# Four single-bank PSUM tiles in place of two double-bank ones, from the end of the attention on

## The chip, the cores and the metric

The kernel runs on one core of one Trainium2 chip. What counts is the device time of one execution in microseconds. The core's engines are TensorE (PE: matmuls, with PEld for its weight loads), VectorE (DVE), ScalarE (ACT), GpSimd (POOL) and SyncE (SP, which here only issues DMAs). TensorE writes its sums into PSUM, of which the kernel uses eight banks of 128 partitions by 512 floats; VectorE and ScalarE read them out.

## What is computed

Attention with capped scores, then two feed-forward layers, all in float32:

```python
scores = cap * tanh(q @ k.T / sqrt(64) / cap)        # 4 x 12 heads, 448 x 448
x = softmax(scores) @ v                              # -> 1792 tokens x 768
h = x @ w_in;  y = (h * cos(h)) @ w_out              # 768 -> 2048 -> 768
a, b = y @ w1, y @ w2                                # 768 -> 1024 each
out = ((a * b) @ w3) @ w_out2                        # 1024 -> 1024 -> 768
```

The product of w3 and w_out2 is formed in the kernel (`make_w34`), so that the last line is one product.

## The kernel before

Every float32 product is made of three matmuls of split operands (`mm3`, lines 378 to 381: high by high, high by low, low by high); a sum collects in one PSUM bank over several `mm3` and is then read out by VectorE or ScalarE. Transposed activations have 448 columns, one batch entry at a time.

The program is written as a list of operations with due times, operands and costs (`Plan.op`), and `Plan.schedule` (lines 191 to 288) works out from them one order for each engine. The order is fixed when the program is built; on the chip an engine takes its list in order, and an instruction waits where its data or its buffer isn't ready. Buffers come from rings: a `Ring` keeps a heap of free slots with the time from which each is free, gives out the one free longest, and takes it back with the end of its last use (lines 236 to 267).

PSUM is held by three rings. Lines 439 to 441 open two tiles of two banks each, `double0` and `double1`, and four tiles of one bank, `bank4` to `bank7`; the list `banks` names the halves of the doubles 0 to 3. `s_r` gives out whole doubles, for the attention's scores: `c_S` (line 590) writes both halves, and `c_exp` (line 602) reads both at once with a Tanh and an Exp (line 607). `pv_r` holds two single banks for the attention's products with v, `hy_r` two for all else. `Plan.move` (line 177) hands a slot from one ring to another: it waits in the plan until the source ring has a free slot, takes it, and puts it, or the slots that `to` names, into the other ring's heap. When the attention ends, `columns` (lines 668 to 670) hands each double to `hy_r` as two banks, as soon as that double is free, and the last `pv_r` bank too; one bank of `pv_r` has gone over earlier (line 667). From then on `hy_r` has all eight banks, four of which are halves of doubles, and Ref-s to them are views of a double (line 440).

The stages overlap: `make_w34` beside the attention, then `moe1` (first layer, units of `mm_h` and `y_part`), begun beside the attention's second half, then `moe2`. `moe2` runs two passes p = 0 and p = 1 over pairs of batch entries. In each, `ab_step` (line 1170) makes, for one block of 128 of the 1024 columns, the two products a and b of two batch entries with seven half-size products (`PRODUCTS`: A11, A12, S2, S1, S3, S4, A22, nine matmuls each) in two banks in turn: products 0, 2, 4, 6 go into p1, 1 into p2, 3 and 5 into p3, each time after the bank was read out (`out` copies, `tt` adds, lines 1183 to 1209). Between them stand the pieces of `o_unit` (line 1213): six sums `acc[m]` that stay in six banks over all eight blocks, three matmuls for each and block. So `ab_step` works with two banks while six are held. In the first pass the right factors (`rights`, line 1123) are converted from raw words first (`convert`, line 819); in the second they are loaded ready.

Pools of tiles are opened and closed in a fixed nesting; the pool `psum` stays open from start to end (lines 437 and 1275).

Of the kernel before, what the change touches and what calls it, by code (L numbers as in the profile page):

```python
# [11 lines left out]
F32 = mybir.dt.float32  # L12
# [4 lines left out]
PSUM = bass.MemoryType.PSUM  # L17
DRAM = bass.MemoryType.DRAM

P = 128  # L20
# [114 lines left out]
class Plan:  # L135
# [38 lines left out]
        self.ops.append(o)  # L174
        return o

    def move(self, src, dst, due, to=None):

        o = Op(due, [(None, 0.0, None)], 0, None)
        it = src.new()  # L180
        it.first = o
        o.allocs.append(it)
        o.move = dst, to or (lambda k: (k,))
        self.ops.append(o)

    def event(self, f, after, before):
        o = Op(-1.0, [(None, 0.0, f)], 0, None)
        self.events.append((o, after, before))
        self.ops.append(o)
# [122 lines left out]
def tile_kernel(tc, *args):  # L312


    nc = tc.nc
    cap = args[3]
    program(tc, *args)
    with tc.tile_pool(name="large", bufs=1) as p:
        c = p.tile([1, 2], F32, name="cap2")
        large = p.tile([1, 1], mybir.dt.int32, name="large")  # L320
        nc.sync.dma_start(c[:, 0:1], cap.rearrange("(o n) -> o n", o=1))
        nc.vector.tensor_scalar(c[:, 1:2], c[:, 0:1], -1.0, None, op0=ALU.mult)
        nc.vector.tensor_tensor(c[:, 0:1], c[:, 0:1], c[:, 1:2], op=ALU.max)
        nc.vector.tensor_scalar(large, c[:, 0:1], CAP_MAX, None, op0=ALU.is_gt)
        with tc.If(nc.values_load(large[0:1, 0:1], min_val=0, max_val=1) > 0):
            program(tc, *args, general=True)
# [3 lines left out]
def program(  # L330
# [12 lines left out]
    general=False,  # L343
# [4 lines left out]
    plan = Plan()  # L348
# [38 lines left out]
    pools = {}  # L387

    def pool(name, **kw):
        pools[name] = Pool(tc, name, {} if general else PADS, **kw)  # L390
        return pools[name]

    right = dict(side="right", reuse_waits="tile")
    for name, kw in dict(const={}, xring={}, dram=dict(space=DRAM), psum=dict(space=PSUM), attn={}, lp={},
                         wi=dict(side="right"), wp=dict(side="right"), yp=right, hp=right, mp=right, cv=right,
                         q2=right).items():
        pool(name, **kw)
# [16 lines left out]
    class Scratch:  # L414
# [7 lines left out]
        def at(self, sub, pick=None):  # L422
            return Ref(self.item, sub, pick)
# [12 lines left out]
    for n in ("const", "xring", "dram", "psum", "attn", "wi", "wp"):  # L436
        pools[n].open()
    psum = pools["psum"].pool
    doubles = [psum.tile([P, 2, 512], F32, name=f"double{n}", bufs=1) for n in range(2)]
    banks = [d[:, n, :] for d in doubles for n in range(2)]  # L440
    banks += [psum.tile([P, 512], F32, name=f"bank{n}", bufs=1) for n in range(4, 8)]
    if general:
        s_r, pt_r, pv_r, hy_r = Banks((0, 1)), Banks((2, 3)), Banks((4, 5)), Banks((6, 7))
    else:
        s_r, pv_r, hy_r = Doubles((0, 1)), Banks((4, 5)), Banks((6, 7))
# [65 lines left out]
    def a_load(i, g):  # L511
        b, h = divmod(i, H)
        qk[i] = A["qr"].new(), A["kr"].new()
        for it, src in zip(qk[i], (q2, k2)):
            for j in range(2):
                r = it.at(j, rows(j))
                dma(at(g) if i else -99.0, r, lambda src=src: src[b, h // 2].rearrange("(i d) s -> d i s", i=2),
                    w=[r], kb=230)
# [6 lines left out]
    def a_split(i, g):  # L525
        q, k = (Ref(x) for x in qk.pop(i))
        qh, ql, ks = (A[x].ref() for x in ("qh", "ql", "ks"))
        copy(at(g), ks, k, 2 * S, "PAD")
        low = Ref(ks.item, None, rows(1))
        lo(at(g), low, k.view(rows(1)), low, 2 * S)  # L530
        copy(at(g), qh, q, 2 * S, "PAD")
        lo(at(g), ql, q, qh, 2 * S)
        for j in range(2):
            st[i + j] = qh[:, j], ql[:, j], ks[:, j]
# [23 lines left out]
    def of_head(f, lag, g, n):  # L558
        i, c = divmod(g - lag, n)
        if c == 0 and 0 <= i < NH:  # L560
            f(i, g)

    def of_pair(f, lag, g, n):
        i, c = divmod(g - lag, n)
        if c == 0 and 0 < i < NH and i % 2 == 0:
            f(i, g)

    def each(f, lag, g, n):
        if 0 <= g - lag < n * NH:
            f(*divmod(g - lag, n), g)  # L570
# [7 lines left out]
    def c_consts():  # L578
        for j in range(2):
            r = A[f"v{j}"]  # L580
            for _, k in r.free:
                POOL.memset(r.tile(k)[:, :, 1 - j, :], 1.0)
# [68 lines left out]
    def columns():  # L651
        c_consts()
        a_load(0, -2)
        a_split(0, -1)
        for g in range(-8, NT * NH + 16):
            of_pair(a_load, -G["ql"], g, NT)
            of_head(cv_load, -2, g, NT)
            of_pair(a_split, -G["qs"], g, NT)
            each(c_S, 0, g, NT)
            each(c_exp, 0, g, NT)  # L660
            each(c_PV, 2, g, NT)
            of_head(c_move, 4, g, NT)
            of_head(c_sums, 4, g, NT)
            of_head(c_norm, 8, g, NT)
            of_head(a_out, 9, g, NT)
            if g == NT * G["hsw"] + 4:
                plan.move(pv_r, hy_r, at(g))
        for _ in range(2):
            plan.move(s_r, hy_r, at(g), lambda k: (2 * k, 2 * k + 1))
        plan.move(pv_r, hy_r, at(g))  # L670


# [591 lines left out]


    (queries if general else columns)()
    first = make_w34()
    moe2(moe1(*first))
# [3 lines left out]
    for _, f in plan.schedule():  # L1272
        if f is not None:
            f()
    for n in ("q2", "hp", "yp", "wi", "lp", "psum", "dram", "xring", "const"):
        pools[n].close()


# [40 lines left out]
```

## Time and profile before

| | |
|---|---|
| median of three runs | 1130.2 us |
| lowest, highest | 1128.82, 1131.66 us |
| the profiled execution | 1128.33 us |
| its span, first to last instruction | 1126.5 us |
| granted TensorE clock, mean | 0.997 |

The page of the profile gives busy times by engine and the longest waits; the trace behind it gives every instruction with its start, its length, the idle time of its engine just before it and what ended that idle time (the releaser). Names stand without buffer numbers: `double<-yS2h,xh` is a matmul into a half of one of the two doubles, `bank<-...` one into a single bank. L379 to L381 are the three matmuls of `mm3`, L355 and L356 copies and casts, L365 two-operand operations of VectorE or GpSimd. Matmuls overlap: each is shown with 0.36 us, but they start 0.20 us apart when nothing holds them.

### The profile page before, as it was taken

The page shows a single profiled execution, that of the slowest core. Times are in us where ns is not written, and L with a number is a line of the kernel's source. Part 1 is how long each engine was busy: PE and PEld are TensorE (multiplying, and loading weights), DVE is VectorE, ACT ScalarE, POOL GpSimd, SP SyncE. Part 2 cuts the span into 40 slices and gives each one's busy share as a digit, 9 for nine tenths or more (in the row PEclk, how much of TensorE's full clock was granted, in tenths as well). Part 3 has the DMA queues.
Part 4 walks back from the last instruction along what each step waited for, and adds up shares of the span by engine and source line. Part 5 has one row for each costly group of instructions (what it writes and reads, how often), then busy time and mean ns, then how long its engine had stood idle before and what let it go on. Part 6 is the DMA issues. An engine that isn't in the chain of part 4 may idle for free.

```text
span 1126.5 us, 14022 instructions
## 1 busy us (share of the span) xinstructions
PE 1085.0 (96%) x5040; PEld 933.7 (83%) x5040; DVE 879.0 (78%) x1338; ACT 503.6 (45%) x663; POOL 157.9 (14%) x153
## 2 busy tenths in 40 slices
PE   5999999999999999999999999999898999999997
PEld 3777777778888888889999999999777779899996
DVE  6888767798998898688889877788877769677642
ACT  5887767777756666632243211122323125321121
POOL 2222111222231210110002100011312000000000
PEclk9999999999999999999999999999999999999999
DMA  9885775868757745427633311116443426321232
GB/s 249 223 230 141 209 190 171 238 179 240 202 159 215 220 111 166 160 69 241 229 104 107 127 49 41 52 52 240 154 161 124 143 64 227 134 85 48 67 103 82
DMA packets 95554, 169.04 MB, mean 150 GB/s; under 512 B 37362, under 2 KB 68850, under 8 KB 95474
## 3 DMA queue, kind: packets, MB, share of 16 engines
q1 hardware_dynamic: 95474, 168.05, 49.7%
q8 instruction: 41, 0.67, 0.3%
q14 instruction: 39, 0.32, 0.1%
HBM read 129.30 MB, written 38.62 MB: 149 GB/s over the span
## 4 chain that ended last, share of the span: by engine, by line
PE 81%; DVE 11%; DMA 4%; issue 1%; ACT 1%; SPq 1%; POOL 0%; DVEq 0%; ACTq 0%; POOLq 0%
PE bank L380 12%; PE bank L379 12%; PE bank L381 12%; PE double L379 11%; PE double L380 10%; PE double L381 10%; PE bank L618 9%; PE double L597 3%; PE double L598 2%; DMA kr<-in_k 2%; DVE y L365 2%; DVE w L365 1%; DMA rb<-rs_d 1%; SPq L375 1%; DVE xl L365 1%
## 5 line engine op out<-in xcount | busy, mean ns | idle before, releaser
L618 PE MATMUL bank<-p,v 112*128 112x448 f32 x384 | 161.1, 542 | 0.5 <-issue 0.5
L607 ACT ACTIVATE double<-double,ts 112x896 f32<-112x896 f32 x96 | 93.9, 979 | 62.5 <-PE double L598 62.3
L379 PE MATMUL bank<-xh,wih 128*128 128x448 f32 x270 | 107.6, 399 | 1.4 <-DVE xh L356 1.4
L618 PEld LDWEIGHTS bank<-p,v 112*128 112x128 f32 x384 | 72.3, 189 | 41.0 <-issue 38.4
L379 PE MATMUL bank<-g,woh 128*128 128x448 f32 x260 | 100.6, 387 | 0.8 <-DVE y L356 0.8
L380 PE MATMUL bank<-xl,wih 128*128 128x448 f32 x270 | 97.9, 362 | 0.2 <-DVE xl L365 0.2
L381 PE MATMUL bank<-xh,wil 128*128 128x448 f32 x270 | 97.8, 362 | 0.0
L607 ACT ACTIVATE p<-double,pac 112x896 f32<-112x896 f32 x96 | 96.8, 1011 | 2.1
L381 PE MATMUL bank<-g,wol 128*128 128x448 f32 x260 | 94.2, 362 | 0.0
L380 PE MATMUL bank<-g,woh 128*128 128x448 f32 x260 | 94.1, 362 | 0.0
L365 DVE TENSOR_TENSOR y<-bank,y 128x448 f32<-128x448 f32 x111 | 68.5, 617 | 25.7 <-PE bank L381 24.9
L597 PE MATMUL double<-qh,ks 128*112 128x448 f32 x192 | 72.7, 379 | 13.8 <-DVE ks L365 9.7
L355 ACT COPY hs<-double 128x448 f32<-128x448 f32 x40 | 21.4, 534 | 130.9 <-PE double L381 122.9
L598 PE MATMUL double<-ql,ks 128*112 128x448 f32 x192 | 71.2, 371 | 0.0
L355 ACT COPY hs<-bank 128x448 f32<-128x448 f32 x43 | 23.0, 534 | 84.4 <-PE bank L381 84.2
L379 PEld LDWEIGHTS bank<-xh,wih 128*128 128x128 f32 x270 | 50.7, 188 | 10.1 <-issue 4.5
L380 PEld LDWEIGHTS bank<-xl,wih 128*128 128x128 f32 x270 | 50.7, 188 | 8.8 <-issue 5.2
L379 PE MATMUL bank<-w2h,w3h 128*128 128x384 f32 x128 | 57.4, 448 | 0.0
L379 PEld LDWEIGHTS bank<-g,woh 128*128 128x128 f32 x260 | 48.8, 188 | 8.1 <-issue 2.2
L380 PEld LDWEIGHTS bank<-g,woh 128*128 128x128 f32 x260 | 48.8, 188 | 6.5 <-issue 3.3
L832 POOL TENSOR_SCALAR wx<-rawc 128x768 f32<-128x768 f32 x29 | 30.9, 1066 | 164.0 <-DVE wil L365 72.0
L381 PEld LDWEIGHTS bank<-xh,wil 128*128 128x128 f32 x270 | 50.6, 188 | 3.3
(276 smaller groups left out, 2841.5 us busy)
## 6 DMA issues: line engine op xcount, KB each, us to landing
rawc<-in_w_out SPq DMA_DIRECT2D x16, 768.0 KB, 5.5
stq<-w_d SPq DMA_DIRECT2D x32, 384.0 KB, 3.5
qr<-in_q SPq DMA_DIRECT2D x48, 224.0 KB, 4.8
kr<-in_k SPq DMA_DIRECT2D x48, 224.0 KB, 4.6
rawc<-in_w_in SPq DMA_DIRECT2D x13, 768.0 KB, 5.8
raw<-in_w3T SPq DMA_DIRECT2D x16, 512.0 KB, 5.5
rawl<-in_w SPq DMA_DIRECT2D x10, 768.0 KB, 4.8
raw<-in_w_out SPq DMA_DIRECT2D x8, 768.0 KB, 6.2
```

The lines of the kernel that those rows point to most:

```text
L355: "A": ("ACT", (0.051 if psum else 0.094) + n / 1200, lambda: ACT.copy(dst(), src())),
L365: "D": ("DVE", 0.068 + n / 960, lambda: DVE.tensor_tensor(dst(), a(), b(), op=op))
L375: plan.op(due, [("SP", 0.66, lambda: SP.dma_start(dst(), src()))], r=r, w=w, kb=kb)
L379: PE.matmul(out, wh, xh, start=first, stop=False, skip_group_check=on)
L380: PE.matmul(out, wh, xl, start=False, stop=False, skip_group_check=on)
L381: PE.matmul(out, wl, xh, start=False, stop=last, skip_group_check=on)
L597: PE.matmul(o, w, qh(), start=True, stop=False)
L598: PE.matmul(o, w, ql(), start=False, stop=True)
L607: lambda f=f, x=x, o=o: ACT.activation(o(), s(), f, scale=x[:CP]))],
L618: PE.matmul(pv()[:, :S], w()[:, 2 * c + n].rearrange("p a d -> p (a d)"), p()[:, n, :], start=c == 0 and n == 0, stop=c == NT - 1 and n == 1)
L832: lambda: POOL.tensor_scalar(x(), h_().bitcast(F32), 0.0, 1.0, op0=ALU.mult, op1=ALU.mult)),
```

## The change

`psum` keeps the four single banks. The doubles move into a pool of their own, `doubles`. At the end of the attention the two doubles are handed over together: the first move takes a double and gives nothing on; the second takes the other, depends on the first, gives `hy_r` the banks 0 to 3, and runs `part_doubles`, which closes the pool `doubles` and opens a pool `singles` with four tiles of one bank each under the numbers 0 to 3. `Plan.move` gets a function to run and operations to come after, and returns its operation. In the general case (a cap over 40, not run here) the four single tiles are opened at once.

```diff
-    def move(self, src, dst, due, to=None):
-
-        o = Op(due, [(None, 0.0, None)], 0, None)
+    def move(self, src, dst, due, to=None, f=None, after=()):
+
+        o = Op(due, [(None, 0.0, f)], 0, None)
+        o.deps.update(after)
...
         self.ops.append(o)
+        return o
...
-    doubles = [psum.tile([P, 2, 512], F32, name=f"double{n}", bufs=1) for n in range(2)]
-    banks = [d[:, n, :] for d in doubles for n in range(2)]
-    banks += [psum.tile([P, 512], F32, name=f"bank{n}", bufs=1) for n in range(4, 8)]
+    banks = {n: psum.tile([P, 512], F32, name=f"bank{n}", bufs=1) for n in range(4, 8)}
+
+    def singles():
+        pools["singles"].open()
+        banks.update({n: pools["singles"].pool.tile([P, 512], F32, name=f"bank{n}", bufs=1) for n in range(4)})
+
+    if general:
+        singles()
+    else:
+        pools["doubles"].open()
+        doubles = [pools["doubles"].pool.tile([P, 2, 512], F32, name=f"double{n}", bufs=1) for n in range(2)]
+
+    def part_doubles():
+        pools["doubles"].close()
+        singles()
+
...
-        for _ in range(2):
-            plan.move(s_r, hy_r, at(g), lambda k: (2 * k, 2 * k + 1))
+        first = plan.move(s_r, hy_r, at(g), lambda k: ())
+        plan.move(s_r, hy_r, at(g), lambda k: range(4), part_doubles, [first])
         plan.move(pv_r, hy_r, at(g))
...
-    for n in ("q2", "hp", "yp", "wi", "lp", "psum", "dram", "xring", "const"):
+    for n in ("q2", "hp", "yp", "wi", "lp", "singles", "psum", "dram", "xring", "const"):
         pools[n].close()
```

## Rows read from the trace of the kernel before

**Rows 1.** The page's first part: busy us, share of the span, instructions of each engine

```profile
PE 1085.0 (96%) x5040; PEld 933.7 (83%) x5040; DVE 879.0 (78%) x1338; ACT 503.6 (45%) x663; POOL 157.9 (14%) x153
```

**Rows 2.** Stretches: us; busy PE, PEld, DVE, ACT, POOL; clock; DMA share; GB/s

```profile
495.00:785.77 290.77, 288.89 (x1442) 269.54 (x1440) 239.54 (x390) 75.43 (x114) 29.69 (x25) 1.00 0.38 123
785.77:807.29 21.52, 18.77 (x92) 16.53 (x90) 17.90 (x25) 7.59 (x11) 6.23 (x5) 1.00 0.46 156
807.29:925.21 117.92, 107.01 (x487) 88.47 (x487) 85.78 (x126) 29.56 (x47) 17.90 (x17) 1.00 0.39 129
925.21:988.23 63.02, 62.07 (x306) 57.25 (x307) 51.34 (x87) 28.89 (x52) 1.39 (x2) 1.00 0.49 165
988.23:1085.60 97.37, 97.37 (x487) 91.13 (x486) 61.31 (x99) 18.33 (x30) 2.06 (x4) 1.00 0.20 62
```

**Rows 3.** TensorE's waits, whole run: who for whom, us, times, longest

```profile
PE double L379 <- DVE y L365: 7.8, 10, 2.0
...
PE double L379 <- DVE hs L365: 3.2, 3, 1.7
...
PE bank L379 <- DVE xh L356: 1.4, 1, 1.4
...
PE double L379 <- DVE w L365: 1.2, 4, 0.6
...
PE double L379 <- DVE hs L356: 0.9, 2, 0.7
...
PE bank L379 <- DVE y L356: 0.8, 1, 0.8
...
PE double L380 <- DVE g L365: 0.7, 1, 0.7
```

**Rows 4.** Timeline, first pass, PE, ACT, DVE: start, us, instruction [idle before <-releaser]

```profile
847.75 0.36 PE L381 MATMUL double<-yA11h,xl 128*128 128x448 f32 x1
...
849.55 0.36 PE L381 MATMUL double<-yA12h,xl 128*128 128x448 f32 x1
...
849.94 0.54 ACT L355 COPY w<-double 128x448 f32<-128x448 f32 x1 [2.87 <-PE double L381]
...
850.15 0.36 PE L381 MATMUL bank<-ab,w34l 128*128 128x448 f32 x1
...
850.51 0.62 DVE L365 TENSOR_TENSOR y<-double,w 128x448 f32<-128x448 f32 x1 [0.65 <-ACT w L355]
...
851.19 0.47 PE L379 MATMUL double<-yS2h,xh 128*128 128x448 f32 x1 [0.69 <-DVE y L365]
...
851.50 0.36 PE L380 MATMUL double<-yS2l,xh 128*128 128x448 f32 x1
```

**Rows 5.** Timeline, second pass, the same step

```profile
1006.07 0.36 PE L381 MATMUL double<-yA11h,xl 128*128 128x448 f32 x1
...
1006.47 0.53 ACT L355 COPY w<-double 128x448 f32<-128x448 f32 x1 [1.74 <-PE double L381]
...
1008.67 0.36 PE L379 MATMUL double<-yS2h,xh 128*128 128x448 f32 x1
...
1008.75 0.62 DVE L365 TENSOR_TENSOR y<-double,w 128x448 f32<-128x448 f32 x1
```

**Rows 6.** VectorE, first pass: timeline of a right factor; its longest row of waits

```profile
832.03 2.50 DVE L365 TENSOR_TENSOR xl<-stq,xh 128x768 fp32r<-128x768 f32 x2
...
DVE w L365 <- PE double L381: 12.7, 6, 3.2
```

**Rows 7.** Timeline around the hand-over, ACT and PE

```profile
483.65 1.01 ACT L607 ACTIVATE p<-double,pac 112x896 f32<-112x896 f32 x1
...
488.04 0.71 PE L379 MATMUL double<-g,woh 128*128 128x448 f32 x1
```

**Rows 8.** Timeline at the second pass's start, DVE and PE

```profile
951.02 0.95 DVE L365 TENSOR_TENSOR xl<-stl,xh 128x768 fp32r<-128x768 f32 x1
...
954.41 0.36 PE L379 MATMUL bank<-yA11h,xh 128*128 128x448 f32 x1
```

More of the change, by code (lines that the diff above doesn't have):

```diff
@@ L393, in program @@
     right = dict(side="right", reuse_waits="tile")
-    for name, kw in dict(const={}, xring={}, dram=dict(space=DRAM), psum=dict(space=PSUM), attn={}, lp={},
+    for name, kw in dict(const={}, xring={}, dram=dict(space=DRAM), psum=dict(space=PSUM), doubles=dict(space=PSUM), singles=dict(space=PSUM), attn={}, lp={},
                          wi=dict(side="right"), wp=dict(side="right"), yp=right, hp=right, mp=right, cv=right,
```

## The prediction

> **What bounds the kernel now.** I read the page's head first. TensorE is busy 96% of the span and VectorE 78% [rows 1], so the kernel ends with TensorE's list, and only time in which TensorE stands still can be won. Next the table by stretches, to see where it stands still [rows 2]. Two stretches decide the case, 807.29 to 925.21 and 988.23 to 1085.60. Each is six rounds of the same work: the seven products of `ab_step` (nine matmuls each) and six groups of three matmuls of `o_unit`, 81 matmuls a round, 487 in either row. The later one takes 97.37 us with TensorE never idle, 0.200 us a matmul. The earlier one takes 117.92 us. The difference, 20.55 us, is time that TensorE loses in the first pass (p = 0) and not in the second (p = 1). The granted clock is 1.00 in both, so the clock doesn't make it.
>
> Third, the list of waits [rows 3]. Here the names count. Where TensorE stands before the first matmul of a sum that goes into a half of a double, it waits for whoever reads a sum: 7.8 us for the addition into y, 3.2 us for hs, 1.2 us for w, and there are three more rows of the kind (0.9, 0.7 and 0.7 us, of which one stands). Where it goes into a single bank there are two waits in all, 1.4 and 0.8 us, for operands (xh, and y of one case). Both kinds of banks come from one ring, `hy_r`, and are emptied by the same operations; yet only halves of doubles make TensorE wait for an emptying.
>
> Fourth, the order of time in one round of the first pass, with the code beside it [rows 4]. `ab_step` puts product 0 (A11) into bank p1, has it copied out, puts product 1 (A12) into p2, adds p2 to the copy, and puts product 2 (S2) into p1 again. A11's last matmul ends at 847.75 + 0.36 = 848.11, but the copy of p1 starts at 849.94, just after A12's last matmul at 849.55 + 0.36 = 849.91: it waited for the other bank's product, though ScalarE was idle. The addition that reads p2 then runs 850.51 to 851.13, and S2, which writes p1 and needs only the copy (done at 850.48), starts at 851.19, behind that addition. So both directions show an order that the data doesn't ask for: a reader of one half waits for writes into the other, and a write into one half waits for the reader of the other. In the second pass the same three steps show none of it [rows 5]: A11 ends at 1006.43, the copy starts at 1006.47 while A12 runs, and S2 starts at 1008.67, before the addition that reads p2 at 1008.75. The trace leaves buffer numbers out. `acc` holds six banks in both passes, so two are left for the products; I infer that in the first pass these two are the halves of one double, and in the second they are not.
>
> **The change part by part.** (1) Four tiles in place of two. An order between the two halves then has nothing to hang on, whichever banks the plan draws. What goes: in the stretch of the first pass 117.92 - 97.37 = 20.55 us. In 785.77 to 807.29, 92 matmuls at 0.200 us are 18.4 us of 21.52, so 3.1 us. In 495 to 785.77, 1442 matmuls are 288.4 of 290.77, so 2.4 us; of that the wait for g (0.7 us, an operand, [rows 3]) stays. A stop costs more than its idle time: in [rows 4] the steps 850.15 to 851.19 and 851.19 to 851.50 are 0.84 and 0.11 us over 0.20, together 0.95 for 0.69 us shown. So the wait for g costs 1.0 us, and 1.4 us goes. In 925.21 to 988.23, 306 matmuls are 61.2 of 63.02, so 1.8 us. Sum: 20.55 + 3.1 + 1.4 + 1.8 = 26.8 us, the most that can go. The waits bound it from the other side: 14.5 us in the six rows of this kind, with 21 stops, and 0.26 us more for each, 20 us; shorter stops aren't listed.
>
> (2) What is late next. Operands first: the right factor of the S2 at 851.19 was ready by 832.03 + 2.50 = 834.53, 16.7 us before [rows 6], and its makers mostly stand behind TensorE, so they move too. A write into p1 or p2 now needs only its own bank emptied. Between the end of a product and the next write into its bank lie one product and one group, 9 + 3 matmuls, 2.4 us; emptying takes 0.62 us [rows 4], which leaves 1.7 us for standing in VectorE's queue. VectorE has 85.78 us of work in the stretch [rows 2] for 97.37 us, 88% where it had 73%; of its idle time 12.7 us is one row of waits for TensorE [rows 6], the largest, and will shrink. Its single steps are up to an us long, so an emptying that meets two of them is late by some tenths. I estimate 0.4 us once a round, 2.5 us given back; the bounds are 0 (the second pass, with VectorE at 63%) and the rival below.
>
> (3) The hand-over. Before, each double gives two banks when its own last user is done; now all four come with the second. The last Exp that reads a double ends at 483.65 + 1.01 = 484.66, and the first other use of a double is at 488.04 [rows 7]. So both are free 3.4 us before any is wanted: cost 0 while that holds. If it held the banks until the attention's last product is read out (some 495.6 on the same list), the price lies between 0 and 7.5 us; I take 0, since the code ties it to the doubles' users and not to `pv_r`. The plan counts banks, not tiles, and picks by time; with enough free ones the order stays the same and only numbers change. Closing and opening issue nothing on an engine that the trace before shows, and no DMA is moved past another.
>
> At one place a rule speaks against this gain. The row to weigh it by is the first pass's stop of about 0.7 us, round after round, with two banks for the products. The Trainium skill, Perfetto Trace Analysis, section Optimization Strategy, says that the same gap repeating can mean too little PSUM for the next tile; by that rule the change, which adds no bank, would give nothing. The second pass, which has two banks as well and no gap, speaks against the rule here. The same page, section Matmuls, has groups rotate through different banks so that emptying one overlaps the next; halves of a double do rotate, and [rows 4] show no overlap.
>
> **The sum.** 26.8 - 2.5 = 24.3 us. The profiled execution took 1128.33 us around a span of 1126.5; without 24.3 it is 1104.0. The median shown is 1.9 us above the profiled execution, so against the median it is 1130.2 - 24.3 = 1105.9: I say 1106.
>
> **The rivals.**
> VectorE becomes the bound of the first pass. For: 88% of work with fixed order; the second pass begins just behind it, with the lower half of its first factors at 951.02 + 0.95 = 951.97 and the product at 954.41 [rows 8], 2.4 us of room after a stretch in which VectorE is busy 51.34 of 63.02 us [rows 2]. Against: the factors lie 16.7 us ahead [rows 6], and what VectorE makes for the second pass starts, as now, with the first pass's end. If it kept half of its 32.1 us idle, six rounds would take 85.8 + 16.0 = 101.8 us, 4.5 us over TensorE's own, and with 4 us at the start of the second pass the time is 1130.2 - 26.8 + 8.5 = 1112.
> The change doesn't do what it says: the stops come from two banks being too few beside VectorE's load, not from the doubles. Then 1130, within 3 us. For: VectorE is busier in the first pass. Against: [rows 4], where the copy waits with ScalarE idle.
> Slower: the hand-over. If the four banks came only behind the last product, the plan would be made anew from 488 on with three banks for 7.5 us, and if the order that comes puts a product directly behind its own bank's emptying (0.95 us a time, some 25 of them would undo the gain) the time is 1130.2 + 7.5 = 1138. It decides only from that many on; in [rows 7] nothing points to it.
>
> **How the numbers follow.** Forecast (1103 to 1109) 0.70, VectorE as the bound (1109 to 1118) 0.22, no change 0.05, slower 0.03. The range reaches from all 26.8 us and a us and a half of spread in the runs to a little past the first rival's 1112: 1101 to 1115. About 0.3% (3.4 us) is what a measurement of this kernel can tell from none: faster 0.92, same 0.05, slower 0.03.
>
> **What would show it.** Right: no wait of TensorE for y, hs or w before a half's or bank's first matmul beyond some tenths; the rounds of the first pass near 16.3 to 16.7 us instead of 19.7; the copy of p1 starting under 0.1 us behind its own product; TensorE without a gap around 480 to 500. Wrong: rounds that stay near 19 us, or VectorE without idle time there and TensorE waiting for w34l, xl or ab; or a gap before the second pass's first product.

## The result

| | before | after |
|---|---|---|
| median of six runs | 1129.51 us | 1102.41 us |
| lowest | 1128.15 us | 1101.0 us |
| the profiled execution | 1128.33 us | 1101.39 us |
| its span | 1126.5 us | 1099.6 us |
| ratio, after to before | | 0.9756 (95% interval 0.9739 to 0.9772) |

One of the six executions of after took 5645.82 us; it counts in the median (1102.30 us without it), the ratio leaves it out, and what held it up isn't known.

The kernel is 27.1 us faster by the medians, and the span is 26.9 us shorter. The head of the page of after, answering [rows 1]:

```profile
span 1099.6 us, 14038 instructions
...
PE 1075.0 (98%) x5040; PEld 938.1 (85%) x5040; DVE 882.5 (80%) x1338; ACT 505.2 (46%) x663; POOL 157.2 (14%) x153
```

TensorE is busy 1075.0 us instead of 1085.0, and 98% of the span instead of 96%. It runs the same 5040 matmuls. (A matmul that is held up is shown longer, 0.47 us instead of 0.36, so the busy time falls too.) What TensorE waits for, over the whole run, answering [rows 3]: who for whom, us in total, times, longest.

```profile
PE double L612 <- DVE ks L367: 10.0, 1, 10.0
PE double L612 <- ACT p L622: 4.1, 2, 2.1
PE bank L382 <- DVE g L367: 0.9, 1, 0.9
PE bank L381 <- DVE y L358: 0.9, 1, 0.9
PE bank L633 <- issue: 0.4, 1, 0.4
```

These are all its rows. No wait for y by L367, hs or w is left. The first two rows belong to the attention's start, g is an operand, and y by L358 is the copy that empties the bank that TensorE writes next, at 242.8 us, while the attention still holds the other banks. The same stretches as in [rows 2], placed by the same matmuls: 802.62 to 900.10 and 961.37 to 1058.75 are six rounds of the first and of the second pass. Columns as there.

```profile
495.00:784.27 289.27, 288.33 (x1441) 269.87 (x1440) 241.15 (x390) 75.64 (x114) 29.06 (x25) 1.00 0.38 123
784.27:802.62 18.35, 18.32 (x91) 16.80 (x90) 17.51 (x24) 7.63 (x11) 5.50 (x5) 1.00 0.49 171
802.62:900.10 97.48, 97.48 (x487) 91.06 (x486) 86.11 (x126) 30.14 (x46) 19.84 (x17) 1.00 0.48 158
900.10:961.37 61.27, 61.27 (x307) 57.37 (x307) 51.88 (x88) 29.50 (x53) 1.26 (x3) 1.00 0.52 171
961.37:1058.75 97.38, 97.38 (x487) 91.14 (x486) 61.54 (x99) 18.07 (x30) 2.06 (x4) 1.00 0.19 62
```

The first pass's six rounds take 97.48 us instead of 117.92, and TensorE is busy for all of them, as in the second pass. One step of a round, answering [rows 4]:

```profile
836.79 0.36 PE L383 MATMUL bank<-yA11h,xl 128*128 128x448 f32 x1
...
837.19 0.54 ACT L357 COPY w<-bank 128x448 f32<-128x448 f32 x1 [0.30 <-PE bank L383]
...
838.59 0.36 PE L383 MATMUL bank<-yA12h,xl 128*128 128x448 f32 x1
...
839.06 0.62 DVE L367 TENSOR_TENSOR y<-bank,w 128x448 f32<-128x448 f32 x1 [0.38 <-PE bank L383]
...
839.39 0.36 PE L381 MATMUL bank<-yS2h,xh 128*128 128x448 f32 x1
```

A11's last matmul ends at 836.79 + 0.36 = 837.15 and the copy of p1 starts at 837.19, while A12 still runs; S2 starts at 839.39, although the addition that reads p2 has then run only 0.33 us of its 0.62. It is now the picture that [rows 5] showed for the second pass. And the hand-over, answering [rows 7]: the last Exp of the attention, and the first matmul after the attention's product at that place.

```profile
484.01 1.01 ACT L622 ACTIVATE p<-double,pac 112x896 f32<-112x896 f32 x1
...
488.39 0.71 PE L381 MATMUL bank<-g,woh 128*128 128x448 f32 x1
```

In the stretch 478 to 500 us TensorE is busy 22.00 of 22.00 us. The lists of instructions of TensorE, ScalarE and GpSimd are the same in both kernels but for the numbers of the banks; on VectorE three tiny operations on the cap, and on SyncE two stores, stand a few places from where they stood. So no other order made the gain.

### The profile page after: what moved, and what is told of

The parts are those of the page before. It is cut to its first block, busy times and chain, and to the rows that moved or that the text cites. A ratio compares the mean times of both kernels' runs of the same rounds, so it can differ in the third digit from the quotient of the medians.

```text
span 1099.6 us, 14038 instructions
## 1 busy us (share of the span) xinstructions
PE 1075.0 (98%) x5040; PEld 938.1 (85%) x5040; DVE 882.5 (80%) x1338; ACT 505.2 (46%) x663; POOL 157.2 (14%) x153
## 4 chain that ended last, share of the span: by engine, by line
PE 83%; DVE 8%; DMA 5%; issue 1%; SPq 1%; POOL 0%; ACT 0%; DVEq 0%; POOLq 0%; ACTq 0%
PE bank L383 23%; PE bank L382 23%; PE bank L381 23%; PE bank L633 9%; PE double L613 2%; PE double L612 2%; DMA raw<-in_w_out 2%; DMA kr<-in_k 1%; DMA rb<-rs_d 1%; SPq L377 1%; DVE x L854 1%; DVE y L367 1%; DMA rs_d<-rs 1%; DVE w L367 1%; DVE x L858 1%
## 5 line engine op out<-in xcount | busy, mean ns | idle before, releaser
L381 PE MATMUL bank<-xh,wih 128*128 128x448 f32 x384 | 148.4, 387 | 0.0
L381 PE MATMUL bank<-g,woh 128*128 128x448 f32 x384 | 145.7, 380 | 0.9 <-DVE y L358 0.9
L382 PE MATMUL bank<-g,woh 128*128 128x448 f32 x384 | 139.2, 363 | 0.9 <-DVE g L367 0.9
L382 PE MATMUL bank<-xl,wih 128*128 128x448 f32 x384 | 139.3, 363 | 0.0
L383 PE MATMUL bank<-g,wol 128*128 128x448 f32 x384 | 139.3, 363 | 0.0
L383 PE MATMUL bank<-xh,wil 128*128 128x448 f32 x384 | 139.2, 363 | 0.0
L367 DVE TENSOR_TENSOR y<-bank,y 128x448 f32<-128x448 f32 x168 | 103.7, 619 | 43.5 <-PE bank L383 42.5
L382 PEld LDWEIGHTS bank<-xl,wih 128*128 128x128 f32 x384 | 72.2, 188 | 10.5 <-issue 5.2
L382 PEld LDWEIGHTS bank<-g,woh 128*128 128x128 f32 x384 | 72.1, 188 | 10.0 <-issue 3.7
L381 PEld LDWEIGHTS bank<-g,woh 128*128 128x128 f32 x384 | 71.9, 187 | 10.1 <-issue 2.4
L383 PEld LDWEIGHTS bank<-g,wol 128*128 128x128 f32 x384 | 72.1, 188 | 4.3
L382 PE MATMUL bank<-ab,w34h 128*128 128x448 f32 x192 | 69.7, 363 | 0.0
L381 PE MATMUL bank<-ab,w34h 128*128 128x448 f32 x192 | 69.7, 363 | 0.0
```

The lines of the kernel that those rows point to most:

```text
L367: "D": ("DVE", 0.068 + n / 960, lambda: DVE.tensor_tensor(dst(), a(), b(), op=op))
L381: PE.matmul(out, wh, xh, start=first, stop=False, skip_group_check=on)
L382: PE.matmul(out, wh, xl, start=False, stop=False, skip_group_check=on)
L383: PE.matmul(out, wl, xh, start=False, stop=last, skip_group_check=on)
```

## The experiments

Five rounds of the first pass, from the first matmul of the third round's A11 (the first one in [rows 2]'s third stretch) to that of the eighth, serve as the measure below; 405 matmuls at 0.200 us are 81.0 us. They take 98.41 us in the kernel before and 81.27 us after. Times are medians, ratios go to runs of the kernel before on the same chip. The runs were made on three chips, and the medians of before there are 1130.1, 1129.5 and 1131.2 us, so differences of two or three us between rows are within the noise. The five rounds of one profile tell more: the three kernels whose first pass is the same give 81.27, 81.27 and 81.26 us.

| kernel | us | ratio (95% interval) | five rounds, us | VectorE busy in them |
|---|---|---|---|---|
| after | 1102.4 | 0.9756 (0.9739 to 0.9772) | 81.27 | 75.07 |
| doubles kept | 1129.7 | 0.9994 (0.9981 to 1.0008) | 100.03 | 74.78 |
| doubles kept, crossed | 1110.1 | 0.9811 (0.9788 to 0.9834) | 82.06 | 74.83 |
| only 2 and 3 single | 1103.0 | 0.9766 (0.9740 to 0.9791) | 81.27 | 74.78 |
| only 0 and 1 single | 1128.9 | 0.9980 (0.9966 to 0.9995) | 99.95 | 74.82 |
| after, 1 step doubled | 1103.1 | 0.9771 (0.9741 to 0.9801) | 82.75 | 78.45 |
| after, 2 doubled | 1105.1 | 0.9789 (0.9759 to 0.9819) | 84.16 | 79.79 |
| after, 4 doubled | 1112.7 | 0.9835 (0.9814 to 0.9856) | 91.50 | 87.50 |
| after, 4 doubled in the second pass | 1104.0 | 0.9777 (0.9748 to 0.9805) | 81.26 | 74.37 |
| before, 4 doubled | 1137.8 | 1.0072 (1.0046 to 1.0098) | 104.71 | 84.40 |

The theory: an order between the two halves of one tile makes TensorE wait. The rivals: the hand-over of all banks at once, the tiles' places in PSUM, or too few banks beside VectorE's load.

**The doubles kept.** Everything of the change stays, the late hand-over and the places included, but the doubles aren't closed.

```diff
     def part_doubles():
-        pools["doubles"].close()
-        singles()
+        banks.update({2 * d + n: doubles[d][:, n, :] for d in range(2) for n in range(2)})
```

> The changed kernel with its late hand-over, its order of instructions and its places in PSUM, but the two double tiles stay open and banks 0, 1 and 2, 3 are again the halves of one double each. Theory (an order between the halves of one double is what costs): the rounds of the first pass take 19.5 to 20 us again, TensorE stops for y, hs and w return, 1126 to 1131 us. Rival (it is the late hand-over of all four banks at once, or where the tiles lie): rounds of 16.3 us, 1101 to 1104 us.

Measured: 1129.7 us, no different from before. The waits of TensorE in this run:

```profile
PE double L381 <- DVE y L367: 7.7, 11, 2.0
...
PE double L381 <- DVE hs L367: 3.2, 3, 1.7
...
PE double L381 <- DVE w L367: 1.2, 4, 0.6
```

These are the rows of [rows 3] again, and five rounds take 100.03 us (98.41 in the kernel before; the clock makes part of the difference, last section). The hand-over and the places are out as causes: they are in this kernel, and it gains nothing. So is the number of banks, which is the same here and after. Two stops of the kernel before are not in this run, though:

```profile
708.33 0.47 PE L379 MATMUL double<-xh,wih 128*128 128x448 f32 x1 [0.71 <-DVE hs L356]
...
979.10 0.47 PE L379 MATMUL double<-yS1h,xh 128*128 128x448 f32 x1 [0.93 <-DVE y L365]
```

The new hand-over gives the banks out under other numbers, so other halves meet, or none; stops of 0.55 and 0.28 us stand at 627.89 and 695.78 instead.

**The doubles kept, crossed.** The same kernel with the four numbers laid across the doubles, so that numbers 2 and 3 (the products' banks in the first pass) are halves of different doubles.

```diff
-        banks.update({2 * d + n: doubles[d][:, n, :] for d in range(2) for n in range(2)})
+        banks.update({d + 2 * n: doubles[d][:, n, :] for d in range(2) for n in range(2)})
```

> As the run with the doubles kept, but the four numbers are crossed over the doubles: 0 and 2 are halves of double 0, 1 and 3 of double 1. The two banks of the products of the first pass (numbers 2 and 3) then lie in different doubles, each beside a bank that holds a sum of o_unit. Theory: products no longer wait for each other's emptying; what is left is that a group of three matmuls into the neighbouring half waits for a reader or holds one up, so 1102 to 1108 us, rounds of 16.3 to 17 us, with two double tiles still there. Rival (two-bank tiles cost in themselves, whichever halves are used): near the 1129 us of before.

Measured: 1110.1 us, 2 us above what the theory gave. The first pass did as expected, 82.06 us for five rounds with two-bank tiles in use (first row; the second is told below):

```profile
811.97:894.03 82.06, 81.64 (x407) 75.78 (x405) 74.83 (x106) 24.93 (x37) 18.83 (x16) 1.00 0.51 169
774.40:777.80 3.40, 3.40 (x11) 2.98 (x11) 1.91 (x3) 0.51 (x1) 1.03 (x1) 0.51 0.53 201
```

So it isn't the two-bank tile in itself that costs, but two halves that are used in turn. The miss lies elsewhere: with this crossing other pairs of sums share a tile in the stage before, and TensorE stops there, most of all here (timeline, just ahead of the first pass):

```profile
771.13 0.37 PE L383 MATMUL double<-g,wol 128*128 128x448 f32 x1
...
773.25 0.61 DVE L367 TENSOR_TENSOR y<-double,y 128x448 f32<-128x448 f32 x1
...
773.92 0.47 PE L381 MATMUL double<-g,woh 128*128 128x448 f32 x1 [2.42 <-DVE y L367]
```

TensorE ran out at 771.5 and started at 773.92, behind an addition that reads the other half (the plan gives TensorE number 0 here and the addition number 2); VectorE had done other work in between. Four stops of this kind, 5.5 us in all, stand in that stage. Which halves meet is decided by the order in which banks come free, and it was not foreseen for that stage.

**One double split at a time.** At the hand-over the pool opens one double and two single tiles; first numbers 2 and 3 are single, then 0 and 1.

```diff
     def part_doubles():
         pools["doubles"].close()
-        singles()
+        pools["singles"].open()
+        d = pools["singles"].pool.tile([P, 2, 512], F32, name="double2", bufs=1)
+        banks.update({n: d[:, n, :] for n in range(2)})
+        banks.update({n: pools["singles"].pool.tile([P, 512], F32, name=f"bank{n}", bufs=1) for n in range(2, 4)})
```

> The changed kernel, but at the hand-over one double-bank tile (numbers 0 and 1) and two single-bank tiles (2 and 3) are opened. Theory: the first pass runs its products in 2 and 3, so its 20.5 us are gained whole, and what is left of the old stops is what the halves 0 and 1 cost in the stage before and in the second pass: 1.1 us at 708 us, 1.3 at 979, a little around 925 and 790, 3 to 6 us in all, so 1104 to 1109 us. Rival (all four must be single for the gain): 1115 us or more.

> The counterpart of the run that left numbers 0 and 1 in one tile: here 0 and 1 are single and 2 and 3 stay the halves of one double. Theory (the first pass runs its products in 2 and 3, and nearly the whole gain is there): rounds of 19.5 to 20 us in the first pass, the stops of the stage before and of the second pass in halves 0 and 1 gone, 1123 to 1128 us. Rival (the gain is spread over both doubles): 1113 to 1119 us.

Measured: 1103.0 us with 2 and 3 single, and 1128.9 us with 0 and 1 single. Five rounds of the first and of the second of these kernels:

```profile
802.83:884.10 81.27, 81.27 (x407) 75.86 (x406) 74.78 (x106) 25.30 (x37) 19.13 (x16) 1.00 0.51 171
```

```profile
810.88:910.83 99.95, 90.69 (x405) 75.03 (x405) 74.82 (x106) 24.77 (x38) 17.30 (x16) 0.98 0.40 136
```

Nearly all of the gain is in the one tile whose halves the first pass uses in turn. Splitting the other alone is worth 0.2%, and its 1128.9 us are just above the 1123 to 1128 that I expected. Leaving the other whole costs 0.6 us by the medians, which is within the noise and less than the 3 to 6 us that I expected: the stops at 708.33 and 979.10 don't come back. They are missing with both doubles kept as well, where the first pass is as late as before, so they hung on the numbers that the old hand-over gave out.

**More work for VectorE.** In `rights`, the differences t1 to t4 (384 columns, 0.55 us as VectorE shows them, 0.47 from one start to the next) are issued twice, in the same place, without the plan's knowledge. The second issue writes the same values again. `times` is 2 for t4 alone, for t3 and t4, for all four; then for all four with p == 1; and for all four in the kernel before. GpSimd makes some of them, so that 6, 10, 24, 32 and 24 steps were added on VectorE.

```diff
-            "D": ("DVE", 0.068 + n / 960, lambda: DVE.tensor_tensor(dst(), a(), b(), op=op))
+            "D": ("DVE", 0.068 + n / 960, lambda: [DVE.tensor_tensor(dst(), a(), b(), op=op) for _ in range(times)])
...
-            tt(due - 1, t4, b21, t2, HALF, ALU.subtract, "PD")
+            tt(due - 1, t4, b21, t2, HALF, ALU.subtract, "PD", times=2 if p == 0 else 1)
```

> The changed kernel with one of the four half-width differences done twice in the first pass (about 0.5 us more of VectorE's work a round, some 4 us in eight rounds). With four doubled the time rose by 10.3 us for some 12 us of work. If VectorE's room in these rounds is small but there (75 of 81 us busy in five rounds): 0 to 2 us over 1102.4. If every added step goes straight to the end: 3.5 to 4.5 us.

> As the run with one doubled, with two of the four differences: about 1 us more of VectorE's work a round, 7 to 8 us in all. If there is room first and then each step counts: 2 to 5 us over 1102.4. If straight to the end: 6 to 8 us.

> The changed kernel with each of the four half-width differences of rights (384 columns, about 0.47 us each on VectorE) done twice in the first pass, in the same place of the list, unknown to the plan: about 1.8 us more of VectorE's work a round, 97 of 97.4 us in six rounds. Theory that VectorE had room to spare, which is why nothing of the gain was given back: 3 to 9 us over 1102.4, since the tightest emptying had 0.07 us to spare. If VectorE is far from the bound: under 1 us. If it was the bound already: 15 us more.

> The changed kernel with all four differences doubled in the second pass instead of the first: the same added work where VectorE is busy 63% of the time. Theory (the rounds of the first pass are at the edge of VectorE, those of the second are not): under 2 us over 1102.4, all of it at the start of the second pass, where there are 2.4 us of room. Rival (added VectorE work costs about its length anywhere, since emptyings stand in its list): 8 to 12 us.

> The kernel before with all four differences doubled in the first pass. There VectorE is idle for 32 of 118 us. If the halves' order alone sets the pace of the first pass and VectorE follows: 0 to 3 us over the 1130 of before. If VectorE's steps stand on the path there too, since TensorE waits for each emptying in turn: 5 to 12 us.

Measured, over the 1102.4 of after: 0.7, 2.7 and 10.3 us for one, two and four (the last over the 9 that I gave as the most), 1.6 us in the second pass. Of these only the 10.3 are clear of the noise; for the others the stretches decide. The kernel before became 8.3 us slower. Five rounds with one and with four doubled:

```profile
802.29:885.04 82.75, 81.98 (x406) 75.69 (x405) 78.45 (x111) 24.98 (x37) 18.67 (x16) 1.00 0.50 168
```

```profile
805.47:896.97 91.50, 85.14 (x406) 76.47 (x405) 87.50 (x125) 24.61 (x37) 19.83 (x16) 0.98 0.47 157
```

From one to four doubled, VectorE's work in five rounds grows by 9.05 us and the rounds by 8.75 (1.3 us of it from the clock, last section). So the first steps cost less than half of their length (1.48 us for 3.38 us of work), and most of each further one goes to the end, though VectorE is idle for 4.0 of 91.50 us even then. How a stop comes about, with four doubled:

```profile
855.92 1.67 POOL L369 TENSOR_TENSOR stq<-stl 128x384 f32<-128x384 f32 x1 [4.15 <-DVE stl L858]
...
856.62 2.48 DVE L367 TENSOR_TENSOR stq<-stl,stl 128x384 f32<-128x384 f32 x2
...
859.03 0.61 DVE L367 TENSOR_TENSOR hs<-bank,hs 128x448 f32<-128x448 f32 x1
...
859.70 0.47 PE L381 MATMUL bank<-wih,xh 128*128 128x448 f32 x1 [1.99 <-DVE hs L367]
```

The emptying into hs stands behind two steps that take 2.48 us together while GpSimd works, and TensorE waits 1.99 us for it. In the second pass the rounds take none of the added work (second row); what is lost is lost ahead of it, where VectorE has 59.44 us of work in 63.15 (first row):

```profile
900.00:963.15 63.15, 61.87 (x307) 56.91 (x305) 59.44 (x102) 28.91 (x52) 1.02 (x2) 1.00 0.51 165
963.15:1044.29 81.14, 81.14 (x407) 75.94 (x405) 64.90 (x106) 16.35 (x26) 2.05 (x4) 1.00 0.21 69
```

And in the kernel before, where VectorE is idle for 20 of 104.71 us, the added work still costs 6.3 us in five rounds:

```profile
810.84:915.55 104.71, 89.17 (x405) 73.75 (x405) 84.40 (x123) 25.04 (x38) 16.71 (x16) 1.00 0.38 130
```

With products that wait for each emptying in turn, a late emptying is on the path however idle VectorE is over the stretch. That an idle share says little of the room holds in both kernels.

## Why the prediction was right

The time was said to be 1106 us, and it is 1102.4, within the range of 1101 to 1115; the forecast mechanism is the one that the runs show. The time lies 0.6 us below the 1103 to 1109 us that had 0.70 of the chances, for the reason given under the second step. By its steps:

- **What goes.** The sum of 26.8 us holds term by term, by the four stretches. First pass 20.55 us, found 117.92 - 97.48 = 20.4. From 785.77 to 807.29 it was 3.1, found 21.52 - 18.35 = 3.2. In the stage before 1.4, found 785.77 - 784.27 = 1.5. From the first pass's end to the second's third round 1.8, found 63.02 - 61.27 = 1.75. Together 26.9, the difference of the spans. The pace of the second pass, the same work without the stops, was the right measure for the first. About 2 us of the two smaller terms, the stops at 708.33 and 979.10, are also gone with the doubles kept: there the size was right, but the new numbers alone would have done it.
- **What is late next.** Here the term was mis-sized: 2.5 us were to be given back, and 0.1 was (97.48 us against 97.38 in the second pass). These 2.4 us are most of what lies between 1106 and 1102.4; the median of before came out 0.7 us lower besides. I had priced 0.4 us for a late emptying in every round. The share of VectorE's work was right (88%: 86.11 of 97.48 us), and so was the room of 1.7 us for an emptying, but in six rounds one emptying outlasted it, and barely:

```profile
818.00 1.35 POOL L369 TENSOR_TENSOR stq<-stl 128x384 f32<-128x384 f32 x1 [4.45 <-DVE stl L858]
...
818.37 1.39 DVE L367 TENSOR_TENSOR stq<-stl,stl 128x384 f32<-128x384 f32 x1
...
819.99 0.61 DVE L367 TENSOR_TENSOR y<-bank,w 128x448 f32<-128x448 f32 x1
...
820.65 0.19 PEld L381 LDWEIGHTS bank<-yA12h,xh 128*128 128x128 f32 x1 [0.19 <-DVE y L367]
820.67 0.46 PE L381 MATMUL bank<-yA12h,xh 128*128 128x448 f32 x1
...
820.97 0.36 PE L382 MATMUL bank<-yA12l,xh 128*128 128x448 f32 x1
```

  The multiplication by which A22's sum leaves the bank ends at 819.99 + 0.61 = 820.60, and A12 writes into that bank at 820.67. The 0.07 us between are no room to spare, as I took them to be in an expectation above: TensorE starts 0.06 us behind its releaser in real stops too (859.03 + 0.61 = 859.64, and 859.70). The weight load waited for the multiplication, and the second matmul starts 0.30 us behind the first instead of 0.20. That is the 0.1 us. The multiplication stood in VectorE's list behind the step of 818.37, which took 1.39 us beside one of GpSimd's (last section), where the prediction had put single steps at up to an us. That it stayed at one such place is close to luck: with one step a round more, five rounds took 1.48 us longer, with four 10.23.
- **The hand-over** costs 0, as taken: the last Exp ends at 484.01 + 1.01 = 485.02, the moved sum begins at 488.39, and TensorE has no gap. That the order stays the same but for the numbers of banks was right as well.
- **One reading was off.** The 0.8 us of y by L356 in a single bank [rows 3] was put down as an operand. L1002 copies a first sum into y, so it is an emptying, of the same bank, and it is there after as well (0.9 us). A single bank can make TensorE wait for its own emptying too; it does so here and, by 0.1 us, at 820.65. Nor are there only two waits for single banks: the whole list has 0.2 us for xl, an operand, and 0.5 us of issue as well. The sum doesn't rest on either.
- **The halves.** That the first pass worked in the halves of one double and the second not was inferred from the waits. The plan, which is fixed when the program is built, bears it out: from the third round on it gives the products of the first pass the numbers 2 and 3 in turn, the two halves of `double1`, and those of the second pass 1 and 3, halves of different doubles. The runs with the doubles kept and crossed show what it costs: the same two-bank tiles take 18.8 us more in five rounds when the products' banks are one tile (17.1 in the kernel before, at the full clock), and 0.8 us when they are not.
- **The rivals.** No change: out, by the run with the doubles kept beside after. VectorE as the bound: not reached, but it begins just behind the point where the kernel stands; 1112.7 us is what it takes with four steps doubled. Slower by the hand-over: nothing of it is seen.
- **The rule set against it.** The Trainium skill, Perfetto Trace Analysis, section Optimization Strategy, takes the same gap again and again as a possible sign of too little PSUM. Here the trace disagrees: with the same two banks for the products the gap is there in 99.95 and 100.03 us and gone in 81.27.

The two directions of the order (a reader held up by writes into the other half, a write held up by the other half's reader) were not tried apart; how the 20 us divide between them stays open.

## What to carry to other kernels

When TensorE stops for an emptying, ask whether the bank that it writes is the one that is emptied; two banks used in turn belong in two tiles, and a tile that one stage needs whole can be closed and opened in parts for the next. A stretch that does the same work without the stops gives the price better than the sum of the listed waits. What then bounds can't be read from an idle share: add a few steps to the engine in question and see from which on the time follows.

## What was not expected of the hardware

**Behind a stop of 2 us the clock halved, or it did not.** In the run with the doubles kept TensorE stood still for 2.0 us (the longest of its waits for y) just ahead of the third round, and from 809.7 to 813 its granted clock was 0.50, the lower of its two levels (1.2 of 2.4 GHz); the second row:

```profile
808.09:908.12 100.03, 90.77 (x406) 75.09 (x406) 74.78 (x106) 24.75 (x38) 17.31 (x16) 0.98 0.40 136
809.70:813.00 3.30, 3.30 (x11) 2.95 (x10) 2.96 (x4) 0.00 (x0) 1.21 (x1) 0.50 0.97 317
```

11 matmuls stand in these 3.30 us, where 0.20 us each would make 2.2. The kernel before has the same stop (its longest in [rows 3] is 2.0 as well), and the clock stayed at 1.00 over its first pass [rows 2]. In the run with the doubles crossed it fell after a stop of 2.42 us (second row there), with four doubled after 1.99 us (0.50 from 861.0 to 864.3, where 10 matmuls stand in 3.30 us). In the kernel before with four doubled it stayed at 1.00 over its five rounds, with stops of 2.33 us and of 2.89 us in them:

```profile
872.79 0.47 PE L379 MATMUL double<-wih,xh 128*128 128x448 f32 x1 [2.89 <-DVE hs L365]
```

So the length of the stop alone doesn't decide; what does isn't shown. After has no stop of that kind in the stretch, and 1.00 throughout. Whether fewer falls of the clock add to the gain over many runs isn't shown either.

**VectorE's steps stretch beside GpSimd's.** A difference of 384 columns takes 0.55 us on VectorE when GpSimd makes none beside it, as here in after (timeline):

```profile
833.93 0.55 DVE L367 TENSOR_TENSOR stq<-stl 128x384 f32<-128x384 f32 x1
```

The one at 818.37, shown above, took 1.39 us, while GpSimd ran a difference of its own from 818.00 to 819.35. The Trainium skill, SBUF — State Buffer, section Who interferes with whom, says that a VectorE instruction with two inputs in SBUF contends with a GpSimd instruction that reads SBUF. The trace agrees, with 1.39 against 0.55 us, and it is this step that made the one emptying late. It isn't always VectorE that is longer: at 837.27 a difference took 0.54 us, while GpSimd's conversion beside it (836.97) shows 2.45 us (GpSimd's spans are rough), and its others in these six rounds 0.88 to 1.54.
